# Sums of layer two's output weights made during layer one, a wider buffer pool for the sums of g, a new layout of two DRAM tensors, and an earlier fetch of phase two's first operands

## The chip, the cores and the metric

The kernel runs on one core of a Trainium2 chip. The metric is the device time of one execution in microseconds (us); lower is better. The engines that matter are TensorE (PE, matmuls), VectorE (DVE), ScalarE (ACT) and SyncE (SP), whose one queue issues nearly every DMA. Each engine takes its instructions in the order in which the program lists them: an instruction that waits holds up everything behind it on that engine.

## The reference

Windowed causal attention feeds two feed-forward layers of the same shape (2304 tokens, model width 512, hidden width 2048):

```python
attn = softmax(mask(scale * q @ k.T, window=64)) @ v   # 4 x 8 heads, 576 tokens, 64 wide
x    = attn rearranged to (2304, 512)
h = x @ w_in;   g = max(h, 0)**2;        x = g @ w_out    # layer one
h = x @ w_in;   g = max(0.01 * h, h);    y = g @ w_out    # layer two
```

## The kernel before

Every float32 operand of a large product is split into a high and a low part of a faster type (ACT casts the high part, DVE subtracts to get the low one), and each product is three matmuls: high x high, high x low, low x high. The program is a plan: `op` and `dma` note an operation with its engine, cost, due time, the buffers that it reads and writes, and `Plan.order` lists them in the order of a modelled run. That list is fixed when the kernel is built, so the modelled times decide only the order; on the chip every engine works it off in order, with waits where data are not there.

Buffers come from slots by tag. A tag such as `wst` (three buffers of 4 KB per partition) or `g` (two) is handed out strictly in the order in which the plan's code asks for it (`turn`). The rings `w0` and `w1` hold x for layer two and, later, operands; `room` finds a place in them, for one slot of an operation at a time.

**Layer one** runs with the attention beside it. Steps of 512 tokens (`step`) do twelve matmuls into `h` (`ffn1`, L678), ACT and DVE make g from it (L644, L648, L649, L347), twelve matmuls follow into `acc` (`ffn2`, L690). Over the later steps `weight_to_dram` (L418) turns layer two's 32 weight chunks of 128x512 into float32 on ACT and DVE and stores them to DRAM, `wf[m, j]`: m = 0 for w_in, m = 1 for w_out.

**Layer two** uses Strassen's scheme (the seven-product form with t and s sums) on 2x2 blocks. *Phase one* is 24 pairs (`pair`, L879), each of a block row p of w_in (eight) and a third s of the tokens (three); a pair is seven products of six matmuls each, 128x384. `w_in(p)` loads two chunks (L817) into a `wst` buffer, forms four sums s1 to s4 on DVE (L827) in another, and casts both into the `x0` or `x1` buffer. After a pair's products DVE adds into `m` (L903), ACT applies the leaky step (L910), and DVE forms the sums of g in two `g` buffers, ta and tb (L961). `keep` (L918) stores all seven parts of g to DRAM, `gd`. From pair 7 on, with every second pair, `w_out_sums(p)` (L855) does for w_out what w_in does for its weights: two loads, four sums on DVE (L827), and a store of the sums to `ws` (L858).

*Phase two* is three superblocks (`superblock`, L1058) of seven products, each of 48 matmuls. A product needs an operand from `gd` (`operands`: two loads of 768 KB, L1027, cast by ACT L344 and DVE L347) and in the first superblock a weight block (`w_out`, two loads of 512 KB from `wf` or `ws`, L990, cast likewise). The first product's loads go to the rings, the others to the three `m` buffers that phase one uses too.

Of the kernel before, what the change touches and what calls it, by code (L numbers as in the profile page):

```python
# [21 lines left out]
DM = H * D  # L22
DFF = 2048
WIN = 64
P = 128
# [71 lines left out]
class Plan:  # L97
# [21 lines left out]
    def room(self, s):  # L119

        at, held = self.rings[s.tag]
        n = max(4 * s.words(), s.pad)
        if at + n > self.RING[s.tag]:
            at = 0
        over = [h for h in held if h[0] < at + n and h[1] > at]
        if any(h[2].users for h in over):
            return False
        self.rings[s.tag] = [at + n, [h for h in held if h not in over] + [(at, at + n, s)]]
        return True
# [27 lines left out]
    def order(self):  # L157
# [23 lines left out]
        while len(result) < n:  # L181
# [13 lines left out]
            for eng in ("pe", "act", "dve", "pool", "sp"):  # L195
                while ready[eng] and busy[eng] <= now:
# [11 lines left out]
                    ring = [s for s in slots if not s.live and s.tag in self.RING]  # L208
                    if not short:
                        assert len(ring) < 2  # L210
                        short = [s.tag for s in ring if not self.room(s)]
# [82 lines left out]
def build(ctx, tc, qp, kp, vp, w1, w2, caps, ident, out, prm=PRM):  # L294
# [123 lines left out]
    def weight_to_dram(j, m, c, after):  # L418

        cv = slot(ep, "e", [P, DM], I32, 4)  # L420
        float_words(1, j, m, c, cv, after)
        dma(
            c + 2.0, lambda: nc.sync.dma_start(out=wf[m, j], in_=f32(cv.ap)), P * DM * 4,
            [(cv, 0)], [(("wf", m, j), 0)],
        )
# [380 lines left out]
    def blocks(m, p, due):  # L806

        cv = slot(wst, "wst", [P, 4, 256], F32, 3)
        for h in range(2):
            if m == 0:  # L810
                to = lambda h=h: cv.ap[:, 2 * h : 2 * h + 2].rearrange("p a b -> p (a b)")
                src = lambda h=h: wf[0, p + NP * h]
            else:
                to = lambda h=h: cv.ap[:, h : h + 3 : 2]
                src = lambda h=h: wf[1, p + NP * h].rearrange("p (a b) -> p a b", a=2)
            dma(
                due - 8.0, lambda to=to, src=src: nc.sync.dma_start(out=to(), in_=src()), P * DM * 4,  # L817
                [(("wf", m, p + NP * h), 0)],
                [(cv, 2 * h), (cv, 2 * h + 1)] if m == 0 else [(cv, h), (cv, h + 2)],
            )  # L820
# [34 lines left out]
    def w_out_sums(p, due):  # L855
        _, sm_ = blocks(1, p, due)
        dma(
            due + 2.5, lambda: nc.sync.dma_start(out=ws[p], in_=sm_.ap), P * 1024 * 4,  # L858
            [(sm_, k) for k in range(4)], [(("ws", p), 0)],
# [4 lines left out]
    def pair(q, s, p, T, A, last):  # L864
# [90 lines left out]
        ta, tb = (slot(gp, "g", [P, 2, NH], F32, 2) for _ in range(2))  # L955
# [15 lines left out]

    OPERANDS = ("11", "22", "21", "t1", "t3", "t2", "t4")
    HP = NP // 2

    def w_out(a, due):

        halves = []
        for h in range(2):
            raw = slot(wst, "wst", [P, HP, 256], F32, 3)
            o = slice(HP * h, HP * (h + 1))  # L980
            if a in SUMS:
                src = ws[o, :, SUMS.index(a)]
                keys = [(("ws", p), 0) for p in range(NP)[o]]
            else:
                i, j = int(a[0]) - 1, int(a[1]) - 1
                src = wf[1, NP * j + HP * h : NP * j + HP * (h + 1), :, 256 * i : 256 * (i + 1)]
                keys = [(("wf", 1, NP * j + p), 0) for p in range(NP)[o]]
            d = due + 2.0 * h
            dma(
                d - 8.0, lambda raw=raw, src=src: nc.sync.dma_start(out=raw.ap, in_=src.rearrange("a p n -> p a n")),  # L990
# [10 lines left out]
    def unit_slots():  # L1001
        for i in range(2):
            u = slot(rings[f"w{i}"], f"w{i}", [P, 2, 1, 2, NH], F32R)
            gunits.append((u, 0))
        for tag in ("x1", "x0"):
            u = slot(xp, tag, [P, 2, 2, 2, NH], F32R)
            gunits.extend([(u, 0), (u, 1)])
# [3 lines left out]
    def operands(s, b, T):  # L1011
# [312 lines left out]
```

## Time and profile before

| | |
|---|---|
| time, median of 3 runs | 846.75 us (843.13 to 849.03) |
| the profiled execution | 844.95 us, of which span 843.2 us |
| PE busy | 828.6 us (98%) |
| DVE, ACT busy | 563.3 us (67%), 462.6 us (55%) |
| DMA | 164.64 MB, mean 195 GB/s |

The span runs from the first to the last instruction. PE's share is of busy time with modelled ends; a stretch in which PE is idle shows as the difference of a window's length and its busy time. Layer one ends at about 483 us, layer two's phase one at about 665 us.

### The profile page before, as it was taken

To read this page: it belongs to the slowest core of one execution; us is meant where nothing else is said; L and a number is where in the kernel's file an instruction comes from. 1 tells how busy PE (TensorE), PEld (TensorE's weight loads), DVE (VectorE), ACT (ScalarE), POOL (GpSimd) and SP (SyncE) were. 2 spreads that over 40 slices of the span, in tenths; PEclk is the share of its full clock that TensorE was granted. 3 is DMA by queue.
4 is the path that set the end of the run, shared out by engine and by line. 5 is a ranking of instruction groups with operands and counts; after the bars stand their busy time and mean duration, and the time that the engine had idled before them with its cause. 6 is when DMAs were issued, how large, how long until landed. Compare 5 with 4: busy or idle time off the path is not lost.

```text
span 843.2 us, 14042 instructions
## 1 busy us (share of the span) xinstructions
PE 828.6 (98%) x5344; PEld 747.9 (89%) x5344; DVE 563.3 (67%) x941; ACT 462.6 (55%) x1011; POOL 0.2 (0%) x4
## 2 busy tenths in 40 slices
PE   9899999999999999999999999999999999999998
PEld 8788988888888888888888899999999989999998
DVE  6988587846655676657887476666664977545453
ACT  5978875545434445435544365555555766444441
POOL 0000000000000000000000000000000000000000
PEclk9999999999999999999999999999999999999999
DMA  9756343325433444436352175867869999767661
GB/s 314 237 191 207 100 150 108 107 79 187 170 136 132 169 137 152 138 126 221 142 176 63 42 248 199 288 243 269 278 243 369 356 373 322 239 206 225 207 206 57
DMA packets 94500, 164.64 MB, mean 195 GB/s; under 512 B 6880, under 2 KB 67040, under 8 KB 94432
## 3 DMA queue, kind: packets, MB, share of 16 engines
q1 hardware_dynamic: 93984, 163.21, 57.6%
q8 instruction: 42, 0.69, 0.3%
q10 hardware_dynamic: 448, 0.52, 0.3%
q14 instruction: 26, 0.21, 0.1%
HBM read 108.66 MB, written 55.05 MB: 194 GB/s over the span
## 4 chain that ended last, share of the span: by engine, by line
PE 83%; DVE 7%; DMA 6%; ACT 2%; issue 1%; SPq 0%; ACTq 0%; DVEq 0%
PE h L678 22%; PE acc L690 21%; PE acc L1058 10%; PE h L879 5%; PE h L1058 4%; PE s L879 4%; PE h L690 3%; PE s L1058 3%; PE acc L879 2%; PE t L1058 2%; DMA m<-gd 2%; PE t L879 2%; PE t L544 2%; PE s L471 2%; DMA wst<-wf 1%; DMA gd<-g 1%
## 5 line engine op out<-in xcount | busy, mean ns | idle before, releaser
L678 PE MATMUL h<-x,w 128*128 128x512 f32 (+1 forms) x1008 | 215.0, 364 | 1.4 <-DVE x L347 1.3
L678 PEld LDWEIGHTS h<-x,w 128*128 128x128 f32 x1008 | 168.2, 189 | 32.1 <-issue 1.7
L690 PE MATMUL acc<-g,w 128*128 128x512 f32 x576 | 141.4, 392 | 0.0
L690 PEld LDWEIGHTS acc<-g,w 128*128 128x128 f32 x576 | 107.2, 188 | 22.0
L879 PE MATMUL h<-w,x 128*128 128x384 f32 x432 | 83.0, 334 | 0.0
L347 DVE TENSOR_TENSOR x<-m,x 128x768 fp32r<-128x768 f32 x54 | 51.0, 957 | 39.7 <-ACT x L344 39.7
L879 PEld LDWEIGHTS h<-w,x 128*128 128x128 f32 x432 | 75.6, 188 | 0.1
L1058 PE MATMUL acc<-x,w 128*128 128x384 f32 x348 | 70.6, 337 | 1.7 <-ACT x L344 1.2
L344 ACT CAST x<-m 128x768 fp32r<-128x768 f32 x54 | 44.6, 836 | 48.3 <-PE h L1058 24.1
L344 ACT CAST w<-m 128x768 fp32r<-128x768 f32 (+1 forms) x50 | 39.4, 799 | 45.6 <-PE h L678 11.3
L347 DVE TENSOR_TENSOR w<-m,w 128x768 fp32r<-128x768 f32 (+1 forms) x50 | 45.1, 908 | 28.5 <-ACT w L344 28.3
L649 DVE TENSOR_TENSOR e<-e 128x512 f32<-128x512 f32 x48 | 33.1, 690 | 46.1 <-ACT g L648 46.1
L1058 PEld LDWEIGHTS acc<-x,w 128*128 128x128 f32 x348 | 61.7, 190 | 2.3 <-ACT x L344 1.5
L879 PE MATMUL s<-w,x 128*128 128x384 f32 x288 | 58.4, 337 | 2.9 <-DVE m L903 2.9
L377 ACT ACTIVATE wst<-wst 128x512 f32<-128x512 f32 x64 | 42.5, 672 | 23.7 <-DMA wst<-w1b 13.1
L644 ACT ACTIVATE e<-h 128x512 f32<-128x512 f32 x48 | 28.5, 594 | 48.6 <-PE h L678 47.6
L879 PEld LDWEIGHTS s<-w,x 128*128 128x128 f32 x288 | 50.2, 188 | 4.8 <-DVE m L903 4.5
L690 PE MATMUL acc<-x,w 128*128 128x512 f32 x192 | 48.1, 394 | 0.0
L386 DVE SCALAR_TENSOR_TENSOR e<-wst,e 128x512 int32<-128x512 int32 x64 | 44.3, 692 | 1.9
L392 DVE SCALAR_TENSOR_TENSOR e<-wst,e 128x512 int32<-128x512 int32 x64 | 44.1, 690 | 1.5
L503 ACT ACTIVATE u<-u,nm 128x128 f32<-128x128 f32 x64 | 25.0, 391 | 29.5 <-DVE nm L500 29.5
L1058 PE MATMUL acc<-w,w 128*128 128x384 f32 x204 | 40.8, 334 | 0.0
(129 smaller groups left out, 1301.3 us busy)
## 6 DMA issues: line engine op xcount, KB each, us to landing
m<-gd SPq DMA_DIRECT2D x40, 768.0 KB, 4.9
gd<-g SPq DMA_DIRECT2D x48, 384.0 KB, 4.2
gd<-m SPq DMA_DIRECT2D x24, 384.0 KB, 4.4
wst<-w1a SPq DMA_DIRECT2D x16, 512.0 KB, 4.2
v<-vp SPq DMA_DIRECT2D x32, 256.0 KB, 3.2
wst<-w2a SPq DMA_DIRECT2D x16, 512.0 KB, 3.5
wst<-w1b SPq DMA_DIRECT2D x16, 512.0 KB, 4.9
wf<-e SPq DMA_DIRECT2D x32, 256.0 KB, 2.2
```

The lines of the kernel that those rows point to most:

```text
L344: nc.scalar.copy(out=dst, in_=src)
L347: eng.tensor_tensor(out=lo, in0=src, in1=f32(hi), op=ALU.subtract)
L377: nc.scalar.activation(out=top, in_=top, func=AF.Copy, scale=2.0**-112)
L386: nc.vector.scalar_tensor_tensor(out=cv.ap, in0=words(1), scalar=-(1 << 31), in1=cv.ap, op0=ALU.bitwise_and, op1=ALU.bitwise_or,)
L392: nc.vector.scalar_tensor_tensor(out=cv.ap, in0=words(0), scalar=29, in1=cv.ap, op0=ALU.logical_shift_right, op1=ALU.bitwise_or,)
L503: nc.scalar.activation(out=u.ap[:, h, :], in_=u.ap[:, h, :], func=AF.Exp, bias=nm.ap[:, h : h + 1], scale=1.0, accum_out=None if dve_sum e ...
L644: nc.scalar.activation(out=r.ap, in_=hp.ap, func=AF.Relu)
L649: op("dve", dve_cost(n), a0 + 1.4, lambda: nc.vector.tensor_tensor(out=r.ap, in0=r.ap, in1=r.ap, op=ALU.mult), [], [(r, 0)])
L678: nc.tensor.matmul(out=hp.ap, lhsT=wi[:, a, kk, :], rhs=x.ap[:, b, kk, c0 : c0 + n], start=(kk == 0 and m == 0), stop=(kk == KD - 1 and m ...
L690: nc.tensor.matmul(out=a, lhsT=w.ap[:, i, d * P : (d + 1) * P], rhs=g[:, b], start=first and m == 0, stop=last and m == 2, skip_group_chec ...
L879: nc.tensor.matmul(out=ps.ap, lhsT=wc.ap[:, v, k, i * P : (i + 1) * P], rhs=x.ap[:, u, n], start=begin and i == 0 and m == 0, stop=i == 1 ...
L1058: nc.tensor.matmul(out=bank[into][i].ap, lhsT=w.ap[:, v, p, i * P : (i + 1) * P], rhs=u.ap[:, x, e, j], start=begin and n == 0 and j == 0 ...
```

## The change

The `wf`, `ws` and `gd` tensors are laid out anew. `wf` keeps only w_in. `wq[k, partition, p, 256]` holds all eight blocks of w_out (four blocks, then the four sums), and `gd` has the partition ahead of p, so that a load of half an operand is one run of 6 KB per partition instead of four of 1.5 KB, and a load of half a weight block one of 4 KB instead of four of 1 KB. The stores are in pieces: 1 KB each for w_out and its sums.

```diff
-    wf = dp.tile([2, NCH, P, DM], F32, name="wf")
-    ws = dp.tile([NP, P, 4, 256], F32, name="ws")
-    gd = dp.tile([NSB, 7, NP, P, NH], F32, name="gd")
+    wf = dp.tile([NCH, P, DM], F32, name="wf")
+    wq = dp.tile([8, P, NP, 256], F32, name="wq")
+    gd = dp.tile([NSB, 7, P, NP, NH], F32, name="gd")
...
+        def store():
+            if m == 0:
+                nc.sync.dma_start(out=wf[j], in_=f32(cv.ap))
+            else:
+                h, p = divmod(j, NP)
+                to = wq[h : h + 3 : 2, :, p].rearrange("k p n -> p k n")
+                nc.sync.dma_start(out=to, in_=f32(cv.ap).rearrange("p (k n) -> p k n", k=2))
...
-            to = gd[s, k : k + n, p].rearrange("m p n -> p m n")
+            to = gd[s, k : k + n, :, p].rearrange("m p n -> p m n")
...
+            k = BLOCK.index(a)
+            src = wq[k, :, o]
...
+            src = gd[s, k, :, o]
```

The sums of w_out move into layer one, one load each instead of two, as soon as both of their chunks have been stored; `tb` takes a `wst` buffer in 22 of the 24 pairs, and `w_in` of the third block row asks for its buffers one pair earlier:

```diff
     for n, (j, m) in enumerate(order):
...
         weight_to_dram(j, m, c, [("step", t, i)])
+        if n > NCH + 2 and n % 2:
+            w_out_sums((n - NCH - 3) // 2, c + 8.0)
+    w_out_sums(NP - 1, stored_at(len(order) + 2) + 6.0)
...
-        if q in range(7, 23, 2):
-            w_out_sums((q - 7) // 2, T)
...
-        ta, tb = (slot(gp, "g", [P, 2, NH], F32, 2) for _ in range(2))
+        ta = slot(gp, "g", [P, 2, NH], F32, 2)
+        tb = slot(gp, "g", [P, 2, NH], F32, 2) if q > NSB * NP - 3 else slot(wst, "wst", [P, 2, NH], F32, 3)
...
+        early = q == 4
+        if early:
+            A[p + 2] = w_in(p + 2, T + span - 3.0)
```

The loads of an operand (`fetch`) are split from its casts (`operands`). The first two operands of phase two and the first two weight blocks are asked for ahead of the last two pairs, both operands into the rings; `room` now places several slots of one operation; and the units that hold cast operands are used in the order x1, w0, w1, x0 instead of w0, w1, x1, x0:

```diff
+        if q == len(seq) - 2:
+            unit_slots()
+            plan.pad = 8192
+            own = [[slot(rings[t], t, [P, HP, NH]) for t in ("w0", "w1")] for _ in range(2)]
+            plan.pad = 0
+            ahead[0, "11"] = fetch(0, "11", t_out - 10.0, own[0], [[o] for o in own[1]])
+            ahead[0, "t1"] = fetch(0, "t1", t_out - 10.0 + 4 * mm12, own[1])
+            wo["11"] = w_out("11", t_out - 9.0)
+            wo["s1"] = w_out("s1", t_out - 5.0)
         pair(q, s, p, T, A[p], q == len(seq) - 1)
...
         def product(a, b, into, begin, end, T, by_bank=False):
-            got = operands(s, b, T)
+            got = operands(ahead.pop((s, b), None) or fetch(s, b, T), T)
```

How the lists move at three places (line numbers shift by 2 to 13 in the change).

DVE in phase one, before: this is the stretch at 555 to 564 us of the trace. L903 adds a product out of PSUM, L961 with 128x768 is ta, the two L961 with 128x384 are tb, and L827 are sums of weights (here `wst_5506`, of w_in).

```order
L903 TENSOR_TENSOR m_5418<-s_131,e_5449 128x384
L903 TENSOR_TENSOR m_5418<-h_198,e_5408 128x384
L827 TENSOR_TENSOR wst_5506<-wst_5470 128x256
L961 TENSOR_TENSOR g_5514<-m_5418 128x768
L827 TENSOR_TENSOR wst_5506<-wst_5506,wst_5470 128x256
L903 TENSOR_TENSOR m_5483<-h_154,e_5516 128x384
L827 TENSOR_TENSOR wst_5506<-wst_5470 128x256
L961 TENSOR_TENSOR g_5540<-m_5418,g_5514 128x384
L961 TENSOR_TENSOR g_5540<-m_5418,g_5540 128x384
L903 TENSOR_TENSOR m_5483<-s_131,e_5495 128x384
```

The same pair's place in the change (L913 answers to L903, L972 to L961), with the pair that follows:

```order
L913 TENSOR_TENSOR m_5462<-h_198,e_5452 128x384
L349 TENSOR_TENSOR x1_5496<-wst_5505,x1_5496 128x1024
L972 TENSOR_TENSOR g_5557<-m_5462 128x768
L972 TENSOR_TENSOR wst_5566<-m_5462,g_5557 128x384
L972 TENSOR_TENSOR wst_5566<-m_5462,wst_5566 128x384
L913 TENSOR_TENSOR m_5546<-s_131,e_5555 128x384
L913 TENSOR_TENSOR m_5546<-h_154,e_5526 128x384
L972 TENSOR_TENSOR g_5597<-m_5546 128x768
```

The second sums stand in `wst` directly behind the first, and no sums of weights stand between them any more.

SP at the turn to phase two, before. L1027 are halves of operands (here the two halves of t1, then of 21), L990 of weight blocks, L918 the stores of g; `m_6470` is the last pair's.

```order
L1027 DMA m_6473<-gd_106 128x4x384
L918 DMA gd_106<-g_6458 128x2x384
L918 DMA gd_106<-m_6470 128x384
L1027 DMA m_6510<-gd_106 128x4x384
L918 DMA gd_106<-g_6499 128x2x384
L990 DMA wst_6532<-wf_104 128x4x256
L918 DMA gd_106<-m_6470 128x2x384
L990 DMA wst_6569<-ws_105 128x4x256
L918 DMA gd_106<-g_6567 128x2x384
L1027 DMA m_6593<-gd_106 128x4x384
L918 DMA gd_106<-g_6591 128x2x384
L1027 DMA m_6614<-gd_106 128x4x384
```

In the change (L1032 operands, L1001 weight blocks, L928 stores; `w1_6342` is the last half of t1, `m_6482` and `m_6521` are the halves of 21, `m_6461` the last pair's):

```order
L928 DMA gd_106<-m_6361 128x2x384
L1032 DMA w1_6342<-gd_106 128x1536
L1001 DMA wst_6465<-wq_105 128x1024
L1032 DMA m_6482<-gd_106 128x1536
L928 DMA gd_106<-m_6461 128x384
L1001 DMA wst_6490<-wq_105 128x1024
L1001 DMA wst_6494<-wq_105 128x1024
L928 DMA gd_106<-g_6463 128x2x384
L1032 DMA m_6521<-gd_106 128x1536
L928 DMA gd_106<-m_6461 128x2x384
L928 DMA gd_106<-g_6545 128x2x384
```

Operand 21's first half stood behind four of the last pair's five stores and now stands ahead of all of them.

DVE in layer one, in the change only: L835 answers to L827 and makes the first sums of w_out, L382 to L394 turn a chunk of weights into float32, L519 to L523 are of the softmax, L657 is g's square.

```order
L394 SCALAR_TENSOR_TENSOR e_3725<-wst_3665,e_3725 128x512
L835 TENSOR_TENSOR wst_3740<-wst_3670 128x256
L519 TENSOR_SCALAR sm_3721<-sm_3721 128x4
L520 RECIPROCAL rc_3750<-sm_3721 128x4
L523 TENSOR_TENSOR u_3709<-u_3709,rc_3750 128x512
L835 TENSOR_TENSOR wst_3740<-wst_3740,wst_3670 128x256
L835 TENSOR_TENSOR wst_3740<-wst_3670 128x256
L835 TENSOR_TENSOR wst_3740<-wst_3670,wst_3740 128x256
```

Before, the four L835 are not there and the rest stands in the same order.

## Rows read from the trace of the kernel before

**Rows 1.** Windows: us, then busy us (instructions) per engine, clock, DMA.
```profile
core 0: us, PE busy (x) PEld busy (x) DVE busy (x) ACT busy (x) POOL busy (x), PEclk, DMA share, GB/s
...
390.00:430.00 40.00, 40.00 (x178) 33.10 (x178) 33.01 (x51) 19.15 (x31) 0.00 (x0) 1.00 0.61 204
...
500.00:530.00 30.00, 29.46 (x169) 28.88 (x168) 22.08 (x36) 20.48 (x43) 0.00 (x0) 1.00 0.62 215
...
560.00:590.00 30.00, 28.25 (x162) 27.61 (x161) 18.41 (x35) 15.85 (x34) 0.00 (x0) 1.00 0.76 272
...
655.00:680.00 25.00, 23.29 (x134) 22.70 (x132) 21.55 (x28) 18.27 (x29) 0.00 (x0) 1.00 1.04 361
680.00:700.00 20.00, 20.00 (x106) 20.00 (x107) 15.58 (x18) 14.35 (x20) 0.00 (x0) 0.91 1.08 370
700.00:760.00 60.00, 60.00 (x348) 60.00 (x347) 35.87 (x42) 30.70 (x41) 0.00 (x0) 1.00 0.77 242
```

**Rows 2.** Waits of PE over the span: total us, times, longest us.
```profile
PE s L879 <- DVE m L903: 2.9, 4, 1.0
```

**Rows 3.** Timeline of PE: start, us, instruction [idle before <-releaser].
```profile
561.80 1.21 PE L879 MATMUL t<-w,x 128*128 128x384 f32 x6
564.00 1.32 PE L879 MATMUL s<-w,x 128*128 128x384 f32 x6 [0.99 <-DVE m L903]
565.16 1.21 PE L879 MATMUL acc<-w,x 128*128 128x384 f32 x6
566.21 1.20 PE L879 MATMUL h<-w,x 128*128 128x384 f32 x6
```

**Rows 4.** Timeline of DVE, the same stretch.
```profile
562.32 1.15 DVE L961 TENSOR_TENSOR g<-m,g 128x384 f32<-128x384 f32 x2 [0.96 <-DMA gd<-g]
```

**Rows 5.** Chain that ended last, from 553 us: start, us, what.
```profile
556.05 6.18 DMA gd<-g
...
579.36 5.63 DMA wst<-wf
...
670.21 7.80 DMA m<-gd
```

**Rows 6.** L961 from 490 to 530 us: what DVE waited for: us, times.
```profile
  ACT m L910: 2.9, 2
```

**Rows 7.** L961 from 530 to 655 us, the same list's first line.
```profile
  DMA gd<-g: 10.8, 9
```

**Rows 8.** L827 from 520 to 660 us: ns min/median/max, first and last start.
```profile
L827 DVE TENSOR_TENSOR wst<-wst x52: 415/422/427, 524.3 to 636.3; 128x256 f32<-128x256 f32 x52
```

**Rows 9.** Timeline of PE at the turn to phase two.
```profile
676.62 0.68 PE L1058 MATMUL acc<-w,w 128*128 128x384 f32 x3
677.14 0.68 PE L1058 MATMUL h<-w,w 128*128 128x384 f32 x3
678.98 0.44 PE L1058 MATMUL acc<-x,w 128*128 128x384 f32 x1 [1.15 <-ACT x L344]
679.97 0.86 PE L1058 MATMUL acc<-x,w 128*128 128x384 f32 x2 [0.55 <-DVE x L347]
...
684.08 0.68 PE L1058 MATMUL s<-x,w 128*128 128x384 f32 x3
```

**Rows 10.** Timeline of one step of layer one.
```profile
425.85 0.63 ACT L648 ACTIVATE g<-e 128x512 fp32r<-128x512 f32 x1
...
427.54 0.69 DVE L347 TENSOR_TENSOR g<-e,g 128x512 fp32r<-128x512 f32 x1
...
430.40 0.62 PE L690 MATMUL acc<-g,w 128*128 128x512 f32 x2
```

**Rows 11.** Waits of ACT from 290 to 470 us.
```profile
ACT wst L377 <- DMA wst<-w2b: 6.4, 2, 3.5
```

**Rows 12.** DMA issues: tensors, count, KB each, median us to landing.
```profile
wf<-e SPq DMA_DIRECT2D x32, 256.0 KB, 2.2
...
x<-e SPq DMA_DIRECT2D x16, 256.0 KB, 2.7
```

More of the change, by code (lines that the diff above doesn't have):

```diff
@@ L117, in __init__, with room @@
         self.pad = 4096
[L119 to L129, printed above, removed]
+    def room(self, slots):
+        rings = dict(self.rings)
+        for s in slots:
+            at, held = rings[s.tag]
+            n = max(4 * s.words(), s.pad)
+            if at + n > self.RING[s.tag]:
+                at = 0
+            over = [h for h in held if h[0] < at + n and h[1] > at]
+            if any(h[2].users for h in over):
+                return s.tag
+            rings[s.tag] = [at + n, [h for h in held if h not in over] + [(at, at + n, s)]]
+        self.rings = rings
     def users_of(self, tags):
@@ L207, in order @@
                     ]
[L208 to L211, printed above, removed]
+                    ring = sorted((s for s in slots if not s.live and s.tag in self.RING), key=lambda s: s.turn)
+                    if not short and ring:
+                        lacks = self.room(ring)
+                        short = [lacks] if lacks else []
                     if short:
@@ L421, in weight_to_dram @@
         float_words(1, j, m, c, cv, after)
[L422 to L425, printed above, removed]
+        def store():
[5 more added lines that the diff above has]
+                nc.sync.dma_start(out=to, in_=f32(cv.ap).rearrange("p (k n) -> p k n", k=2))
+        dma(c + 2.0, store, P * DM * 4, [(cv, 0)], [(("wf", m, j), 0)])
     xt = {}
@@ L857, in w_out_sums @@
         dma(
-            due + 2.5, lambda: nc.sync.dma_start(out=ws[p], in_=sm_.ap), P * 1024 * 4,
-            [(sm_, k) for k in range(4)], [(("ws", p), 0)],
+            due + 2.5, lambda: nc.sync.dma_start(
+                out=wq[4:8, :, p].rearrange("k p n -> p k n"), in_=sm_.ap
+            ),
+            P * 1024 * 4, [(sm_, k) for k in range(4)], [(("ws", p), 0)],
         )
@@ L980, in w_out @@
             o = slice(HP * h, HP * (h + 1))
-            if a in SUMS:
-                src = ws[o, :, SUMS.index(a)]
+            k = BLOCK.index(a)
+            src = wq[k, :, o]
+            if k < 4:
+                keys = [(("wf", 1, NP * (k % 2) + p), 0) for p in range(NP)[o]]
+            else:
                 keys = [(("ws", p), 0) for p in range(NP)[o]]
[L984 to L987, printed above, removed]
             d = due + 2.0 * h
             dma(
-                d - 8.0, lambda raw=raw, src=src: nc.sync.dma_start(out=raw.ap, in_=src.rearrange("a p n -> p a n")),
+                d - 8.0, lambda raw=raw, src=src: nc.sync.dma_start(out=raw.ap, in_=src),
                 P * 1024 * 4, keys, [(raw, 0)],
@@ L1041, in build @@
     mm12 = 12 * mm_cost(NH)
-    wo = {}
+    wo, ahead = {}, {}
     def superblock(s, T, banks):
@@ L1255, in build @@
     A = {p: w_in(p, now - prm["WP"] + 2.0 * p) for p in range(2)}
+    t_out = now + len(seq) * span
     for q, (p, s) in enumerate(seq):
         T = now + q * span
+        early = q == 4
[10 more added lines that the diff above has]
+            wo["s1"] = w_out("s1", t_out - 5.0)
         pair(q, s, p, T, A[p], q == len(seq) - 1)
@@ L1260, in build @@
             x_combos(2, q, T + 9.0)
-        if s == NSB - 1 and p + 2 < NP:
+        if s == NSB - 1 and p + 2 < NP and not early:
             A[p + 2] = w_in(p + 2, T + span - 3.0)
-        if q in range(7, 23, 2):
-            w_out_sums((q - 7) // 2, T)
-    now += len(seq) * span
-    unit_slots()
+    now = t_out
     a, b, e, f = ("acc1", "acc2"), ("acc0", "s"), ("acc3", "h"), ("t", "h")
```

70 lines of the change are left out of this document (36 added, 34 removed).

## The prediction

> **What bounds the kernel now.** I read the windows first, to see in which stretches PE is idle at all [rows 1]. It is not idle in layer one (390 to 430: busy 40.00 of 40) nor in phase two once it runs (700 to 760: 60.00 of 60). Small gaps lie between: 0.54 us at 500 to 530, 1.75 at 560 to 590, 1.71 at 655 to 680, and right behind that the one stretch with a low clock, granted 0.91 on the mean of 680 to 700. So the kernel is bound by PE with a few holes in it, and a change that leaves the matmuls alone can win those holes and no more.
>
> The waits of PE tell what the holes in phase one are: four waits, 2.9 us in all, of a product's first matmul for a DVE addition (L903) that has to empty its bank [rows 2]. The timeline of one of them shows how much more than its idle time it costs: at PE's pace six matmuls take 1.05 us from start to start (565.16 to 566.21), here the group before took 2.20 (561.80 to 564.00) and the next 1.16 [rows 3]. That is 1.26 us lost, 0.27 more than the 0.99 idle, since PE's pipeline fills anew.
>
> DVE's own timeline of that stretch shows why L903 was late: the instruction ahead of it in DVE's order, an L961 that writes the next sums into a `g` buffer, stood 0.96 us for `gd<-g`, the store that still read the buffer [rows 4]. The chain of waits goes the same way. It runs through that store (issued 556.05, landed 6.18 later), in a second stall through another `gd<-g`, and in the other two through a weight load such as the one of 579.36, which took 5.63; then through the load `m<-gd` of 670.21, 7.80 us long [rows 5]. L961 never waits for a store between 490 and 530 us, where only w_in's sums run [rows 6]; from 530 to 655, with w_out's sums in the same queue and on the same DVE, it waits 9 times, 10.8 us together [rows 7]. DVE hides most of this; four times it shows.
>
> **Part one: the stalls of phase one go.** Between 520 and 660 us DVE makes 52 sums of weights of 0.42 us [rows 8]; 32 of them are w_out's (eight blocks of four) and leave, 13.4 us of DVE work out of a stretch of some 125 us. With them leave 4 MB of loads and 4 MB of stores that stood in SP's queue among the stores of g. And tb no longer asks for a `g` buffer, so a store has a whole pair (seven products, 7.3 us) more until its buffer is wanted. I take all four stalls as gone: 2.9 idle and 4 times 0.27 for the refill, 4.0 us. The bounds are 0 (tb now waits for `wst` where it waited for `g`) and 4.0.
>
> What is late next: tb shares the three `wst` buffers with w_in's loads and sums, in strict order, so a load that lands late holds the buffer that tb wants. Two of the four stalls already began with such a load. The other 20 sums are those of five w_in, which stay in this stretch; I charge 1.0 us, with bounds 0 and 2.5 (two stalls like that of 564.00).
>
> **Part two: the head of phase two.** PE starts three matmuls every 0.52 us (676.62 to 677.14). From 677.14 to 684.08 it started 18, which is 3.12 us of work in 6.94: 3.8 us lost [rows 9]. First it waits 1.15 us for ACT's cast and 0.55 for DVE's of the operand 21; then it runs slower than its pace up to 684.08, and the granted clock is at its lower level of 1.2 GHz for part of the 20 us from 680 on [rows 1]. The operand's load was issued at 670.21 and landed at 678.01 [rows 5]. In the change it stands ahead of all five stores of the last pair (before, behind four of them), so it is issued several us earlier. Without the idle time I expect no low clock either: in this trace PE ran at full clock in every other stretch shown. So the whole 3.8 us go. Bounds: 0 and 3.8. Against the whole gain stands the queue: from 655 to 700 the DMA share is 1.04 and 1.08 at 361 and 370 GB/s [rows 1], so the engines are full and what is fetched earlier pushes other loads back. Part of that is made good by the weight sums and stores that no longer lie ahead.
>
> By the page HBM Reference of the Trainium skill (Specifications) a core that streams alone reaches about 425 GB/s. No row here shows over 370, and the row decides; by the page's figure, if the longer runs reached it, the 7.80 us load would take 7.80 x 361 / 425 = 6.6 us by estimate, and the sum would be the same, because the earlier issue already covers it.
>
> **Part three: layer one pays.** The 32 sums, 32 x 0.42 = 13.4 us of DVE, now lie between about 335 and 480 us, eight bursts of four with 1.69 us each. In 390 to 430, DVE has 40.00 - 33.01 = 7.0 us free [rows 1], and two or three bursts (4.2 on the mean) fall there. One burst pushes everything behind it on DVE, among it the low part of g: in the step shown it was done at 427.54 + 0.69 = 428.23, and PE wanted g first at 430.40, so 2.17 us of room against 1.69 [rows 10]. That hides it, if the burst's load has landed and steps are alike. Below: 0. Above: each burst has also to wait for its load, and longest by the 3.5 us that ACT once waited for a weight load there [rows 11]; then 1.69 + 3.5 - 2.17 = 3.0 us show, eight times 24. The order puts a burst about ten us behind its chunk's store, so I am near the low end and take 1.5 us, in two or three places where room is shorter.
>
> **Part four: the layout.** Loads in longer runs gain nothing where PE has no hole: from 700 us on it is never idle at a DMA share of 0.77 [rows 1]. The stores become pieces: a store cut into rows of 2 KB far apart (`x<-e`) lands in 2.7 us, one in whole rows (`wf<-e`) of equal size in 2.2 [rows 12]. The 0.5 us more of each store of w_out is covered by the four `e` buffers, that of gd by the freed `g` buffers. If that cover were gone, the nine waits of [rows 7] would each be 0.5 longer, 4.5 us. I take 0.
>
> The page DMA: Bandwidth & Descriptors of the Trainium skill (Specifications) asks for pieces of at least 512 B for full rate. The old pieces were above that already, so by it too the layout would give nothing; the sum is the same.
>
> **Sum.** -4.0 + 1.0 - 3.8 + 1.5 = -5.3. The profiled execution took 844.95, so 839.6. It stands 1.8 below the median of the three runs (846.75), and those spread over 5.9; if the change's runs lie likewise about theirs, the median would be 841.4. I forecast 840.5, between the two.
>
> **Rivals.**
> (a) More comes back: layer one hides all, w_in's loads stall nothing, and the holes at 500 to 530 close as well (0.5): 844.95 - 4.0 - 3.8 - 0.5 = 836.6. For it: DVE has 7 us free in 40 [rows 1]. Against: other small holes of phase one wait for things that the change does not touch.
> (b) The head only moves: 361 to 370 GB/s is all that the queue gives, another operand or weight block is late in 21's place, and only the 4.0 - 1.0 of phase one count, less layer one's 1.5: 843.5. For it speaks the DMA share over 1; against it, that 8 MB of sums' traffic are gone before.
> (c) Layer one pays more: a burst shows in each of eight places by its overhang and the refill, about 0.7 us: 5.6 in place of 1.5, 843.7. For it: 2.17 - 1.69 leaves only 0.48. Against: no wait in this part of layer one has reached PE so far, not even ACT's 3.5 us [rows 11].
> (d) Slower: the bursts wait for their own loads, DVE in order behind them. From a hold of 2.17 us on, each us is paid eight times; the gains of 6.8 (phase one and head net) are used up at 0.85 us over it, that is a wait of 1.3 us ahead of each burst. At 3.5 us each: 838.15 + 24 = 862. For it: four stalls of just this kind in phase one. Against: the order leaves ten us where such loads take 5.6.
> (e) The moved sums do not matter, since tb waits for `wst` as it did for `g` and the stalls stay: 844.95 - 3.8 + 1.5 = 842.7.
>
> **Chances.** Forecast 0.48, and its own range is 837.5 to 843; (a) 0.20, (b) 0.10, (c) 0.10, (d) 0.06, (e) 0.06. What a measurement of this kernel can tell from no change is about 1%, 8.5 us. Faster by more than that means under 838.3: all of (a), and 0.06 of the forecast's case, 0.26. Slower by over 1%: (d), 0.06. The rest, 0.68, within 1%. The range goes from 835 ((a), less 1.6 for the scatter) to 846 ((b), (c), (e), with 1.8 for the scatter and a little) and leaves out (d) and the far ends, under 0.2.
>
> **What would show it.** Right: between 530 and 655 us no PE wait for DVE's addition behind `gd<-g`, and the second sums' waits on `wst` under 0.5 us; in the window 680 to 700 (shifted) the granted clock 1.00 and PE 20.00 of 20; PE without a hole from 335 to 480 with the sums of w_out in it. Wrong: gaps of PE in layer one with a wait of DVE on `wst<-wq` ahead (c, d); a first matmul of phase two that waits for another cast (b); second sums that wait for `wst<-wf` (e). The forecast falls if the time is over 843 or under 837.5.

## The result and the profile after

| | before | after |
|---|---|---|
| time, median of 18 runs each | 845.88 us (843.13 to 853.06) | 839.25 us (836.77 to 844.16) |
| ratio, with its 95% interval | | 0.9914 [0.9892, 0.9936] |
| the profiled execution | 844.95 us, span 843.2 | 840.72 us, span 838.9 |

The change makes the kernel 0.9% faster. The forecast of 840.5 us (835 to 846) holds it, and so does the range of the forecast's own case. The medians say 6.6 us. The two profiled executions say 4.2, and the part that the change touches says 8.0 between these two: the same matmuls start 3.8 us *later* in the profile after than in that of before, from the first 12 us of the program on, where nothing was changed. That start is told of below, in the part on the start and in the last section; it has to be taken out before anything else is read. So the main measure here is a stage table, worked out from the timelines: the start of the same matmul, counted in PE's order, in one trace and in the trace of before (both have 5344 matmul records), at four places (356.44, 483.26, 650.51 and 703.67 us in the trace of before). Each column is what a stage adds to the distance. Behind 703.67 nothing changes any more; the last matmul starts at 839.39 before and 835.16 after.

| us against before | start | layer one 356 to 483 | phase one 483 to 651 | turn 651 to 704 | from 356 on |
|---|---|---|---|---|---|
| the change | +3.80 | +0.02 | -4.57 | -3.47 | -8.03 |

Of the 3.47 us at the turn, 1.7 are not what a usual execution would win. In the trace of before PE runs at 1.2 GHz for 3.41 us there (680.16 to 683.57), which costs half of that, 1.71 us. The mean granted clock of a timed execution shows whether it had such a stretch: 3.41 us at half clock take 0.002 off it. Of the 71 executions of the kernel before that were timed beside the experiments, 46 have a mean of 1.000, 5 of 0.999 and 20 of 0.997 or 0.998; of the 18 of the change none is under 0.999. So most executions of the kernel before have no such stretch, and against those the change wins about 8.03 - 1.71 = 6.3 us from 356 us on, near to the 6.6 of the medians.

The waits of PE over the span, after (total us, times, longest us). The line of [rows 2], four waits for DVE's addition, is gone, and so are the two waits of [rows 9]:

```profile
PE h L686 <- DVE x L349: 1.3, 2, 0.8
...
PE acc L889 <- ACT acc L346: 0.9, 2, 0.6
...
PE t L889 <- ACT m L920: 0.2, 1, 0.2
```

The windows after, those that answer to [rows 1] (us, then busy us of each engine, granted clock, DMA share, GB/s), the second and third of them moved by the 4 us of the start:

```profile
390.00:430.00 40.00, 40.00 (x206) 32.97 (x205) 34.80 (x59) 19.89 (x33) 0.00 (x0) 1.00 0.81 275
...
504.00:534.00 30.00, 29.66 (x170) 29.21 (x170) 22.42 (x37) 19.66 (x42) 0.00 (x0) 1.00 0.64 224
564.00:594.00 30.00, 30.00 (x175) 30.00 (x174) 16.50 (x28) 17.32 (x37) 0.00 (x0) 1.00 0.64 225
655.00:680.00 25.00, 24.75 (x141) 24.11 (x140) 21.23 (x26) 18.93 (x28) 0.00 (x0) 1.00 1.03 401
680.00:700.00 20.00, 20.00 (x118) 20.00 (x117) 17.10 (x19) 15.93 (x20) 0.00 (x0) 1.00 1.02 418
```

PE is busy 30.00 of 30 where it was 28.25, 24.75 of 25 at the turn where it was 23.29, and the granted clock is 1.00 at 680 to 700 where it was 0.91. Layer one stays at 40.00 of 40 with more DVE work (34.80 against 33.01) and more DMA (0.81 against 0.61). The hole of 504 to 534 stays in the main (0.34 us; 0.54 before).

What DVE waited for ahead of the sums of g (L972) from 530 to 660 us, the only line of that list; the 10.8 us for `gd<-g` of [rows 7] are gone:

```profile
  ACT m L920: 14.2, 23
```

### The profile page after: what moved, and what is told of

It is laid out like the page before. It is cut to its first block, busy times and chain, and to the rows that moved or that the text cites. A ratio compares the mean times of both kernels' runs of the same rounds, so it can differ in the third digit from the quotient of the medians.

```text
span 838.9 us, 14060 instructions
## 1 busy us (share of the span) xinstructions
PE 830.2 (99%) x5344; PEld 751.0 (90%) x5344; DVE 562.7 (67%) x941; ACT 463.7 (55%) x1011; POOL 0.2 (0%) x4
## 4 chain that ended last, share of the span: by engine, by line
PE 89%; DMA 5%; DVE 4%; ACT 1%; issue 0%; SPq 0%; ACTq 0%; DVEq 0%
PE h L686 22%; PE acc L698 21%; PE acc L1071 10%; PE h L889 8%; PE s L889 5%; PE h L1071 5%; PE h L698 3%; PE acc L889 3%; PE s L1071 2%; PE t L889 2%; PE t L1071 2%; PE t L552 2%; PE s L479 1%; DMA gd<-g 1%; PE t L543 1%; DMA w<-vp 1%
## 5 line engine op out<-in xcount | busy, mean ns | idle before, releaser
L1071 PE MATMUL acc<-x,w 128*128 128x384 f32 x360 | 73.8, 334 | 0.1
L349 DVE TENSOR_TENSOR x<-m,x 128x768 fp32r<-128x768 f32 x50 | 47.2, 957 | 36.3 <-ACT x L346 36.2
L346 ACT CAST x<-m 128x768 fp32r<-128x768 f32 x50 | 41.2, 837 | 40.9 <-PE h L1071 17.4
L1071 PEld LDWEIGHTS acc<-x,w 128*128 128x128 f32 x360 | 63.4, 188 | 0.4 <-DVE w L349 0.4
L346 ACT CAST w<-m 128x768 fp32r<-128x768 f32 (+1 forms) x50 | 39.5, 798 | 39.3 <-PE h L1071 10.8
L657 DVE TENSOR_TENSOR e<-e 128x512 f32<-128x512 f32 x48 | 33.1, 690 | 37.9 <-ACT g L656 37.8
L394 DVE SCALAR_TENSOR_TENSOR e<-wst,e 128x512 int32<-128x512 int32 x64 | 44.1, 690 | 1.5
L698 PEld LDWEIGHTS acc<-x,w 128*128 128x128 f32 x192 | 34.6, 189 | 6.3
```

The lines of the kernel that those rows point to most:

```text
L346: nc.scalar.copy(out=dst, in_=src)
L349: eng.tensor_tensor(out=lo, in0=src, in1=f32(hi), op=ALU.subtract)
L394: nc.vector.scalar_tensor_tensor(out=cv.ap, in0=words(0), scalar=29, in1=cv.ap, op0=ALU.logical_shift_right, op1=ALU.bitwise_or,)
L657: op("dve", dve_cost(n), a0 + 1.4, lambda: nc.vector.tensor_tensor(out=r.ap, in0=r.ap, in1=r.ap, op=ALU.mult), [], [(r, 0)])
L698: nc.tensor.matmul(out=a, lhsT=w.ap[:, i, d * P : (d + 1) * P], rhs=g[:, b], start=first and m == 0, stop=last and m == 2, skip_group_chec ...
L1071: nc.tensor.matmul(out=bank[into][i].ap, lhsT=w.ap[:, v, p, i * P : (i + 1) * P], rhs=u.ap[:, x, e, j], start=begin and n == 0 and j == 0 ...
```

## The experiments

All kernels are edits of the changed kernel, and all edits are of the order of work, of buffers or of the layout in DRAM; none leaves out work. Two small parts of the change stay in every one of them and were not tried apart: the earlier `w_in` of the third block row and the new order of the units for cast operands. In o_fetch both are there and phase one wins only 0.82 us, so they are not its cure; for the turn no run bounds them. Their stages, as above, with the timed ratio to the kernel before, run on the same chip:

| kernel | sums of w_out in | tb in | early fetch | layout | start | layer one | phase one | turn | from 356 on | ratio [95%] |
|---|---|---|---|---|---|---|---|---|---|---|
| the change | layer one | wst | yes | new | +3.80 | +0.02 | -4.57 | -3.47 | -8.03 | 0.9914 [0.9892, 0.9936] |
| u_sums | phase one | wst | yes | new | +4.12 | 0.00 | -4.22 | +7.26 | +3.04 | 1.0062 [1.0036, 1.0087] |
| u_tb | layer one | g | yes | new | +0.08 | +0.02 | -4.55 | -3.75 | -8.28 | 0.9902 [0.9874, 0.9929] |
| u_fetch | layer one | wst | no | new | +0.10 | +0.02 | -4.59 | +4.10 | -0.47 | 0.9996 [0.9974, 1.0019] |
| u_layout | layer one | wst | yes | old | -0.23 | -0.01 | -4.46 | -4.15 | -8.62 | 0.9900 [0.9872, 0.9928] |
| o_fetch | phase one | g | yes | new | +3.94 | 0.00 | -0.82 | +2.49 | +1.67 | 1.0016 [0.9983, 1.0048] |
| o_sums | layer one | g | no | new | +7.57 | +0.02 | -4.51 | -3.03 | -7.53 | 0.9950 [0.9922, 0.9977] |
| o_tb | phase one | wst | no | new | +3.74 | 0.00 | -3.97 | +1.60 | -2.37 | 0.9983 [0.9957, 1.0010] |
| min_two | layer one | g | yes | old | +3.80 | -0.01 | -4.39 | -3.83 | -8.24 | 0.9911 [0.9886, 0.9936] |
| s_only | layer one | g | no | old | +5.10 | -0.01 | -4.48 | -2.36 | -6.85 | 0.9929 [0.9897, 0.9961] |
| burst3 | layer one, thrice | wst | yes | new | +0.07 | +5.73 | -3.63 | -2.53 | -0.43 | 0.9992 [0.9966, 1.0018] |

The column of the turn mixes PE's waits with stretches of low clock, and the latter come in some executions of a kernel and not in others. Here they stand apart, between the same two matmuls. Operand 21 is that of the third product, for which PE waits in [rows 9]; the timed executions are those with a mean granted clock of 0.998 or less (their mean does not tell where in the execution the clock was low).

| kernel | turn | PE idle for operand 21, us | PE idle in all, us | at 1.2 GHz, us | timed executions with low clock |
|---|---|---|---|---|---|
| before | 0 | 1.70 | 1.86 | 3.41 | 20 of 71 |
| the change | -3.47 | 0 | 0.18 | 0 | 0 of 18 |
| min_two | -3.83 | 0 | 0.16 | 0 | 0 of 10 |
| o_sums | -3.03 | 0.70 | 0.70 | 0 | 3 of 10 |
| s_only | -2.36 | 1.37 | 1.37 | 0 | 2 of 8 |
| o_tb | +1.60 | 0 | 4.78 | 0 | 9 of 10 |
| u_fetch | +4.10 | 2.16 | 4.90 | 3.41 | 9 of 10 |
| o_fetch | +2.49 | 0 | 4.05 | 3.41 | 4 of 10 |
| u_sums | +7.26 | 0 | 8.89 | 6.82 | 10 of 10 |

### Undoing one part each

**u_sums.** The sums go back to phase one, with the buffer, the fetch and the layout of the change:

```diff
-        if n > NCH + 2 and n % 2:
-            w_out_sums((n - NCH - 3) // 2, c + 8.0)
-    w_out_sums(NP - 1, stored_at(len(order) + 2) + 6.0)
...
+        if q in range(7, 23, 2):
+            w_out_sums((q - 7) // 2, T)
```

> The change with the sums of w_out back in phase one (from pair 7 on, every second pair), all else as in the change. Theory Q (the sums' DMA traffic and DVE work cause the stalls of phase one): with tb still in wst, PE loses 3 to 5 us again between 520 and 660 us, in waits for DVE's addition that stand behind a transfer. Theory B (the third buffer for tb is the cure): less than 1 us is lost there. Layer one in both theories as in the change (no gap).

Phase one: -4.22, so theory B holds there; with tb in `wst` the sums' traffic stalls nothing. The loss came at a place that neither theory had named, the turn: +7.26, and the kernel is slower than before. The timeline of PE shows one wait of 7.75 us for a weight block's cast (L1071 <- L346):

```profile
668.38 1.01 PE L1071 MATMUL acc<-x,w 128*128 128x384 f32 x2 [7.75 <-ACT w L346]
```

Its load was issued at 660.51, and ACT, which casts it, waited for it until 667.28:

```profile
660.51 0.59 SPq L1001 DMA_DIRECT2D wst<-wq  x1
...
667.28 1.04 ACT L346 CAST w<-wst 128x1024 fp32r<-128x1024 f32 x1 [3.80 <-DMA wst<-wq]
```

The chain that ended last (start, us, what) does not hold this wait; it leads to a short one behind it (0.65 us at 680.54), through the last sums' store and then the load of a further weight block, one behind the other, with DMA full:

```profile
661.16 7.51 DMA wq<-wst
...
668.74 9.42 DMA wst<-wq
678.15 0.02 issue
678.18 1.06 ACT w L346
```

**u_tb.** The second sums of g in a `g` buffer again:

```diff
-        tb = slot(gp, "g", [P, 2, NH], F32, 2) if q > NSB * NP - 3 else slot(wst, "wst", [P, 2, NH], F32, 3)
+        tb = slot(gp, "g", [P, 2, NH], F32, 2)
```

> The change with tb in a g buffer again, all else as in the change. Theory Q: without the sums' traffic the stores of g land in time, PE loses under 1 us between 520 and 660 us. Theory B: 3 to 4.5 us are lost there, and the second sums wait for gd<-g again, over 8 us in all.

Theory Q: phase one -4.55, as in the change. DVE waits four times for the store of a `g` buffer, 3.4 us in all against 9 times and 10.8 us before [rows 7], and none of it reaches PE. What DVE waited for ahead of L972, 530 to 655 us:

```profile
  ACT m L920: 8.8, 17
  DMA gd<-g: 3.4, 4
```

**u_fetch.** Only the first operand has its loads in the rings, asked for after all pairs, 10 us later by their due times:

```diff
-            own = [[slot(rings[t], t, [P, HP, NH]) for t in ("w0", "w1")] for _ in range(2)]
...
-            ahead[0, "11"] = fetch(0, "11", t_out - 10.0, own[0], [[o] for o in own[1]])
-            ahead[0, "t1"] = fetch(0, "t1", t_out - 10.0 + 4 * mm12, own[1])
-            wo["11"] = w_out("11", t_out - 9.0)
-            wo["s1"] = w_out("s1", t_out - 5.0)
...
     now = t_out
...
+    own = [slot(rings[t], t, [P, HP, NH]) for t in ("w0", "w1")]
+    ahead[0, "11"] = fetch(0, "11", t_out, own, [[o] for o in own])
```

> The change with only phase two's first operand in the rings, asked for after the last pair as before, and its loads due 10 us later; all else as in the change. Theory F (the place in SP's queue makes the head): PE loses 3 to 4 us around 665 to 690 us, part of it at a granted clock of 1.2 GHz. Theory Q (the queue is shorter without the sums, so the place does not matter): under 1 us.

Theory F by its sign and more by its size: the turn goes from -3.47 to +4.10, 7.6 us, twice what stood in the expectation, and the whole gain is lost. But o_sums below, also without the early fetch, does not lose it. The chain of u_fetch shows what is different: a store of a `g` buffer that DVE waits for, then a cast on DVE and the load of a weight block behind it, then the load of operand 21; the three transfers take 7 to 8 us each, one behind the other:

```profile
644.41 8.10 DMA gd<-g
...
652.52 0.25 DVE g L972
...
653.38 1.23 DVE w L349
...
654.63 7.35 DMA wst<-wq
...
669.38 8.30 DMA m<-gd
677.68 0.02 issue
```

**u_layout.** The old `wf`, `ws` and `gd`, two loads for each block of w_out again:

```diff
-    wf = dp.tile([NCH, P, DM], F32, name="wf")
-    wq = dp.tile([8, P, NP, 256], F32, name="wq")
-    gd = dp.tile([NSB, 7, P, NP, NH], F32, name="gd")
+    wf = dp.tile([2, NCH, P, DM], F32, name="wf")
+    ws = dp.tile([NP, P, 4, 256], F32, name="ws")
+    gd = dp.tile([NSB, 7, NP, P, NH], F32, name="gd")
...
-            src = gd[s, k, :, o]
+            src = gd[s, k, o].rearrange("a p n -> p a n")
```

> The change with the old layout of the three DRAM tensors (loads of operands and weight blocks in pieces of 1.5 and 1 KB, the sums' blocks in two loads), all else as in the change. Theory N (the layout gives nothing): PE's times as in the change within 0.5 us, the rate in the fullest 20 us falls from 418 to about 370 GB/s without PE noticing. Theory L (the higher rate carries the head): PE loses 1 to 4 us around 665 to 690 us.

Theory N: -8.62 in all against -8.03 of the change. The rate does fall, to 385 and 368 GB/s from 401 and 418, and PE is busy 25.00 of 25 and 20.00 of 20 all the same:

```profile
655.00:680.00 25.00, 25.00 (x145) 24.82 (x145) 20.72 (x25) 17.51 (x25) 0.00 (x0) 1.00 1.07 385
680.00:700.00 20.00, 20.00 (x117) 20.00 (x116) 16.31 (x20) 13.70 (x18) 0.00 (x0) 1.00 1.08 368
```

### One or two parts alone

The next kernels are put together from the same edits: o_fetch undoes the sums and tb, o_sums tb and the fetch, min_two tb and the layout. burst3 is in the next part.

> Early fetch and layout alone: sums of w_out in phase one, tb in a g buffer. Theory E (either cure alone is enough for phase one, as undoing one of them has shown no stall there): here both are missing, so PE loses 3 to 5 us between 520 and 660 us as before. Rival R (the new layout, with one load per sum in place of two, was the cure): under 1 us. At the turn to phase two theory E expects a loss of 5 us or more, because the last sums' store and load lie on the path of the weight block s1; in all 848 to 856.

Theory E in phase one, where only 0.82 us are won: the stalls are back when both cures are missing. In the list of what DVE waited for ahead of L972 from 530 to 655 us the line of before is there again, 11.1 us in 9 times, with the new layout:

```profile
  DMA gd<-g: 11.1, 9
```

The loss at the turn was 2.5 us, half of the least that stood in the expectation. 850.29 us is in its range, but by luck: six of the ten runs lie at 850.11 to 851.02, and the profiled one, which is among these, began 3.94 us late.

> Sums in layer one and layout alone: tb in a g buffer, first operands fetched as before. Theory E: phase one loses under 1 us (4.4 won), the turn to phase two loses 6 to 9 us as without the early fetch, so the time is that of the kernel before within 2 us. Rival (the loss at the turn came from tb's wst buffers, which the weight blocks need too): under 4 us lost there, 839 to 842.

The rival holds. With tb in `g` the turn wins 3.03 us without any early fetch, -7.53 in all; 1.71 of it is the low clock that this trace does not have, and PE still waits 0.70 us for operand 21. Timed it was 843.0 in the median, and the profiled execution began 7.57 us late; the four shortest of its ten runs took 837.52 to 839.78.

> Sums in layer one and early fetch alone: old layout, tb in a g buffer. Theory E (these two parts carry the whole gain): PE's times from layer one on as in the change within 1 us. Rival (layout and buffer cover for each other, as one of them alone could be undone without loss): 2 to 5 us lost in phase one or at its end.

Theory E: -8.24 against -8.03, within 0.4 us in each stage.

**s_only** and **o_tb** are the moved sums alone (with tb, fetch and layout undone) and tb alone (with sums and fetch undone, the layout kept).

> The moved sums alone: sums of w_out in layer one; old layout, tb in a g buffer, first operands asked for after the last pair. Theory M (the moved sums are the change; the other three parts only pay for each other): counted from a matmul in layer one, the end comes 7 to 8 us earlier than in the kernel before (4.4 in phase one, 2.5 to 3.5 at the turn). Rival (the new layout carried the turn where the early fetch was missing): 4 to 5 us earlier, all in phase one.

-6.85 in all, 0.15 short of the 7 of theory M: -4.48 in phase one, -2.36 at the turn. The old layout costs at most 0.7 at the turn (against o_sums), and the early fetch wins 1.5 there (min_two against s_only). Most of the -2.36 can't be put down to the moved sums: PE still waits for the casts of operand 21 at the same two matmuls as in [rows 9], 0.82 and 0.55 us in place of 1.15 and 0.55, and 1.71 us come of a clock that stays at 1.00 in this trace, as it does in most executions of the kernel before:

```profile
678.80 0.44 PE L1073 MATMUL acc<-w,w 128*128 128x384 f32 x1 [0.82 <-ACT w L346]
679.79 0.62 PE L1073 MATMUL acc<-w,w 128*128 128x384 f32 x2 [0.55 <-DVE w L349]
...
680.00:700.00 20.00, 20.00 (x116) 20.00 (x116) 17.21 (x19) 14.65 (x19) 0.00 (x0) 1.00 1.08 370
```

The operand's load was issued at 669.07, where it was 670.21 before.

> tb in wst alone, with the layout: sums of w_out in phase one, first operands asked for after the last pair. Theory M: phase one is as good as with the moved sums (4 to 5 us won between 520 and 660 us), but the wst buffers come late for the first weight blocks, 6 us or more are lost at the turn, so 2 us or more slower than before in all. Rival (the buffer is a cure of its own): 3 to 5 us faster than before in all.

Neither. The buffer is a cure of phase one (-3.97), and the turn pays for it, as theory M had it, but 1.6 us and not over 6: 2.4 us faster from layer one on, and the timed ratio cannot be told from 1. PE stood idle for 4.78 us at this turn, and the trace has no low clock there; nine of the ten timed executions have one somewhere, so the 1.6 is likely less than usual.

### Layer one, with three times the sums

```diff
-        combine(0, (cv, 2), (cv, 3), ALU.add, due)
+        for _ in range(3 if m == 1 else 1):
+            combine(0, (cv, 2), (cv, 3), ALU.add, due)
...
```

> The change with every sum of w_out made three times over in layer one (96 DVE operations there instead of 32, 40 us of DVE instead of 13). Theory W (DVE waits for ACT so long in layer one that the sums lie in those waits): PE loses 0 to 4 us between 350 and 490 us. Rival S (a burst counts against the room of one step, 2.2 us): 12 operations are 5.1 us, so 2.9 us lost at each of eight places, 23 us.

5.7 us in layer one: over theory W's 4, and far from the 23 of rival S. Why 32 sums cost nothing shows in what DVE waits for in layer one, first before (331 to 485 us), then after (335 to 489): it stood 22.4 us for ACT's g ahead of g's square, and now 14.8.

```profile
DVE e L649 <- ACT g L648: 22.4, 13, 4.0
```

```profile
DVE e L657 <- ACT g L656: 14.8, 13, 2.4
```

So 7.6 of the 13.4 us of sums can lie in time in which DVE stood for ACT, and the rest in its other idle time; this is read from the totals and was not traced sum by sum. Late loads cost nothing either: in u_layout DVE waited six times, 5.5 us in all, for the load ahead of its sums in this stage, and layer one lost nothing (-0.01). The plan's order, which knows their cost, does not set a burst as one block either: of the eight, several are split over two or three places. With three times the work that wait is down to 5.7 us, and PE waits for DVE's g, 1.9 us of the 5.7; where the rest is lost was not traced:

```profile
DVE e L657 <- ACT g L656: 5.7, 4, 2.4
```

```profile
PE acc L698 <- DVE g L349: 1.9, 2, 1.3
```

### The start

The changed kernel's runs lie in groups: nine at 836.77 to 838.18, six at 840.32 to 841.16, three at 842.10 to 844.16. Windows of the start, before (first) and after, with equal programs up to there, show in the matmuls done what divides them:

```profile
4.00:8.00 4.00, 3.62 (x42) 2.85 (x42) 1.52 (x3) 1.02 (x4) 0.00 (x0) 1.00 1.09 309
8.00:12.00 4.00, 4.00 (x54) 3.59 (x55) 3.86 (x8) 3.21 (x14) 0.00 (x0) 1.00 1.03 407
```

```profile
4.00:8.00 4.00, 3.96 (x26) 3.11 (x27) 1.38 (x2) 0.73 (x2) 0.00 (x0) 1.00 1.04 293
8.00:12.00 4.00, 4.00 (x26) 3.45 (x28) 1.99 (x4) 1.80 (x7) 0.00 (x0) 1.00 1.01 361
```

54 matmuls against 26 in the same 4 us, PE busy in both: it runs at half the pace, that of 1.2 GHz. (The clock column reads 1.00 in all four, for the trace has no record of the granted clock ahead of its first rise.) The first record of full clock stands at 4.32 us in the trace of before and at 16.20 in that of after. Only one execution of each kernel has a trace, so that the groups of runs are early and late starts is a reading; the profiled ones fit it (u_layout 836.09 and u_tb 836.75 with an early start, the change 840.72 and min_two 840.51 with one 3.80 us later). To see whether the kernel decides that, two kernels do more warming matmuls without a gap ahead of the first product, 12 and 18 instead of 7, on top of u_layout (w12's lines are shown; w18 has 11 and 18 in the place of 5 and 12):

```diff
-        for i in range(prm["WARM"]):
+        for i in range(prm["WARM"] + 5):
...
-                "pe", 0.43 if i < prm["NCOLD"] else prm["WC"], prm["WD"],
+                "pe", 0.43 if i < prm["NCOLD"] else prm["WC"], -150.0 if i < 12 else prm["WD"],
```

> The change with the old layout, and with 12 instead of 7 warming matmuls ahead of the first product at the start. Theory G (TensorE's clock rises at the end of the first block of matmuls only if the chip catches it without a gap; else it stays at 1.2 GHz to 13 us or later and everything comes 3 to 7 us later): a longer block without a gap is caught every time, the clock rises before 8 us, every run lies at 837 to 839. Rival C (it is chance, or something outside the kernel): two groups of runs as before, 836 to 838 and 840 to 844, the second a little later by the longer block.

> As the kernel with 12 warming matmuls, with 18. Theory G: one group of runs, 1 us behind that with 12, 838 to 840, clock at full before 9 us. Rival C: two groups, both 2 us later than with 7.

One group each: 839.18 to 840.64 and 840.09 to 840.99, six runs each, and full clock from 4.29 and 5.08 us on, so theory G in this, as far as twelve runs go; its times are missed. The matmuls of 4 to 8 us in w12's trace (first record of full clock at 4.29) are 48:

```profile
4.00:8.00 4.00, 4.00 (x48) 3.58 (x47) 1.38 (x3) 0.35 (x1) 0.00 (x0) 1.00 1.05 314
...
24.00:28.00 4.00, 4.00 (x38) 3.71 (x35) 3.90 (x11) 1.95 (x10) 0.00 (x0) 0.60 0.32 117
```

But the price is higher than the 1 and 2 us in the expectations: their medians are 3.4 and 3.8 us over that of u_layout (836.60 of four runs, on another chip), as much as a late start costs. For w12 the second line shows some of it: a granted clock of 0.60 over 4 us, so 1.6 us lost. Counted without the added matmuls, their traces lose 2.6 and 2.7 us against that of u_layout up to the matmul of 356 us and 1.5 each at the turn; why the turn pays was not followed. So it makes the time steadier and not shorter: 840.03 and 840.43 against 839.25 of the change. Against the kernel before they are at 0.9914 [0.9885, 0.9943] and 0.9921 [0.9892, 0.9949]. That a longer first block is what makes the rise sure is not shown beyond these runs; a kernel that has it without the price was not found.

## The prediction, step by step

**What bounds the kernel: right.** PE's holes were what could be won, and the 8.0 us from layer one on are 4.57 in phase one and 3.47 at the turn, where the prediction had 4.0 and 3.8; 1.71 of the turn is the low clock that most executions of the kernel before don't have.

**The stalls of phase one: right in size, wrong in what each edit is worth.** Term -4.0, measured -4.57: the four stalls, and a small hole of about 0.3 at 533 us of before that the sum had left out; the rest was not traced. But the two edits to which it put them are each enough alone (u_sums -4.22, u_tb -4.55), and with both missing only 0.82 is won (o_fetch). Rival (e), that tb waits for `wst` as it did for `g`, did not come: DVE waits for no store ahead of the second sums, and the 1.0 us charged for it was 0.

**The head of phase two: right for this trace, in size and reason, but not by that edit alone.** Term -3.8, measured -3.47. The step said that operand 21's load would be issued several us earlier and that therefore the wait and the low clock go. The load was issued at 659.78 in place of 670.21, with PE only 0.8 us ahead of its place in the trace of before:

```profile
659.78 0.42 SPq L1032 DMA_DIRECT2D m<-gd  x1
```

The wait is gone wherever the early fetch and the moved sums come together (the change, min_two, u_tb, u_layout, burst3), and it stands, with 0.70 and 1.37 us, where the sums are moved and nothing is fetched early (o_sums, s_only). So the moved sums shorten this wait and the early fetch ends it, worth 0.7 to 1.5 us as long as tb is in `g` (u_tb against o_sums, min_two against s_only). But the early fetch needs the moved sums: with the sums still in phase one it loses (o_fetch +2.49, u_sums +7.26, against 0 of the kernel before and +1.60 of o_tb), and other waits of PE stand in the place of operand 21's. That is what rival (b) foresaw, and the prediction had the sums' part only as something that makes good for crowding. The low clock was luck of the profile: 1.71 of the 3.8 us were in one trace and are not in most executions. That without the idle time it would not come held: of the 36 timed executions of the change, u_tb, u_layout and min_two none has a mean clock under 0.999. But idle time does not have to bring it: s_only kept 1.37 us of the 1.70 and o_tb had 4.78 us at a granted clock of 1.00. With tb in `wst` the early fetch is worth 7.6 us (the change against u_fetch), 1.71 of it low clock: the chain of u_fetch shows stores, casts and loads one behind the other, which fits with the weight blocks' turn at the `wst` buffers; which of the links decides was not tried apart.

**Layer one: mis-sized.** Term +1.5, measured 0.02. It set a burst of 1.69 us against the room of one step, 2.17 us [rows 10]. By the totals most of the sums lie in DVE's waits for ACT instead, and in the change their loads had landed in time. ACT did wait longer for layer one's own weights: 14.1 us in 6 times against the 6.4 of [rows 11], and PE showed none of it. Rivals (c) and (d) fell; at three times the work the price is 5.7 us.

**The layout: right.** 0 in the sum; u_layout gives -8.62 against -8.03. The 0.5 us charged to a store in pieces can't be seen either: the stores `wq<-e` lie between 2.1 and 5.8 us, those of u_layout in whole rows in the same stretch between 2.0 and 6.1.

**The sum.** -5.3 was forecast from the profiled execution, -8.0 is measured from layer one on between the two profiles, where rival (a), with -8.35, is nearer than the forecast. Against an execution of the kernel before without the low clock at the turn it is -6.3, where the forecast is nearer. The 2.5 us too many were charged for layer one and for w_in. That the median came out 1.25 us from the forecast is in part luck: what was charged too much was about made up for by late starts, which the forecast did not know of. In half of the runs the time is 3 us and more above the middle of the nine short ones (837.30). The step from one profiled execution to a median, put at 1.8 us of scatter, hid two things that differ from run to run, a start by 4 us and more, which is in no relation to the change, and a stretch of low clock by 1.7.

**What was to show it**: no wait behind `gd<-g`, a granted clock of 1.00 at the turn and a layer one without holes all came, and still did not tell which edit does what; only undoing the parts one by one did, and at the turn only together with the clock of each trace.

## What to carry to other kernels

Where a queue is crowded in one stage, moving its work to a stage whose engines stand idle for someone else can cure the stall and cost nothing there: the move alone won 4.5 of the 4.6 us of phase one for 0 in layer one. It did not free the head of the next stage by itself; there the wait for an operand went only with the earlier fetch as well, and the earlier fetch without the move lost time. Two edits that cure the same stall are not worth their sum, and one of them (a buffer lent from another pool) can bring a debt elsewhere that a third edit only pays off. The price of work that is put into a stage is to be read from what its engine waits for over the whole stage, not from the room of a single step. Before a stretch of low clock in one trace is counted as something to win, look in how many executions it is there.

## What was not expected of the hardware

**The start of TensorE's clock.** The same first instructions ran at half pace up to 4.3 to 5.0 us in five of the twelve profiles of kernels with seven warming matmuls (the kernel before, u_tb, u_fetch, u_layout, burst3), and up to 13.5 to 23.5 us in the other seven, which costs 3.7 to 7.6 us in the column "start" of the table. None of these kernels decides it: their programs are equal up to there. A single profile against another is therefore no measure of some us; the same matmul in the middle of both is.

**The low clock at the turn.** In the trace of before, PE waited 1.15 and 0.55 us [rows 9], and the granted clock then stood at 1.2 GHz for 3.41 us. In that of s_only it stayed at 2.4 GHz behind waits of 0.82 and 0.55 us for the same matmuls, and in that of o_tb it stayed there through 4.78 us of idle time at the turn. Executions of one kernel differ in it: in those of the kernel before, the mean granted clock is 1.000 in 46 of 71 and 0.998 or less in 20. Four kernels have at most 0.2 us of idle time of PE at the turn in their traces (the change, u_tb, u_layout, min_two); in none of their 36 timed executions is the mean under 0.999. Which executions with such waits get the low clock is open.

**The rate of DMA with longer runs.** From 655 to 700 us the DMA share is 0.98 to 1.08 in all kernels of the first table of experiments and in the kernel before. With pieces of 1.5 and 1 KB the two windows of [rows 1] moved 346 to 385 GB/s (before, s_only, min_two, u_layout), with runs of 6 and 4 KB 401 and 418 in the change, but 352 to 418 over all the kernels with the new layout. So only longer runs reached over 385, and they did not always do so. By the page HBM Reference of the Trainium skill (Specifications) a core that streams alone reaches about 425 GB/s; no window here is over that. By the page DMA: Bandwidth & Descriptors of the Trainium skill (Specifications) pieces of 512 B would be enough for full rate; no run here decides that, as stores and loads are mixed in these windows and none measured one length by itself. The kernel's time did not follow the rate: u_layout is as fast as the change.
